# Start-up of a convolution and channel-mix kernel: mu_k loaded earlier, x in four loads, padding zeroed by GpSimd

## The chip, the cores and the metric

The kernel runs on one core of one Trainium2 chip. The metric is device time in microseconds (us) of one execution. "Span" is the time from the first to the last instruction in the profile of one execution, about 1.7 us less than the device time.

Engines: PE is TensorE, PEld its weight loads, DVE is VectorE, ACT is ScalarE, POOL is GpSimd, SP is SyncE; a q behind a name is that engine's queue. "L453" is line 453 of that kernel; the changed kernel's lines are shifted by some five.

## The reference, cut to what matters

```python
# x: (8, 4160, 192); weight: (8 heads, 7 taps)
w = softmax(weight)                                   # per head
y[b, s] = sum over k of w[h, k] * x_padded[b, s + k]  # 6 zero rows in front of every sequence
y_prev = y shifted by one row
xk = mu_k * y + (1 - mu_k) * y_prev
xr = mu_r * y + (1 - mu_r) * y_prev
k = relu(xk @ w_k)                                    # 192 -> 1024
v = (k * k) @ w_v                                     # 1024 -> 192
out = sigmoid(xr @ w_r) * v
```

## The kernel before

The convolution is a matmul with a banded matrix `toe` that is built on the chip from the softmax of the weights. x comes in blocks of 120 rows with 6 rows of overlap, in groups of up to ten blocks. Group 0 is loaded as float32 by the hardware queues and cast by ScalarE, for GpSimd's loads (which cast on their way) start later (the first issue at 2.38 us, against 0.80 us on the hardware queues). The first six groups are the first pair of sequences; group 5 is the first that ends in a partly filled block.

```python
def x_tile(g, eng):                       # eng is always VectorE in this kernel
    p, blk0, nb, _, _ = groups[g]
    xb = three.tile([P, GB, 2, D], BF16, tag="xb", name="xb")     # ring of three buffers
    xbs[g] = xb
    if blk0 == 0:
        eng.memset(xb[0:32, 0, :, :], 0.0)          # zero rows ahead of a sequence
    elif g > 5:
        eng.memset(xb[0:1, 0, 0, 0:2], 0.0)         # one word: VectorE takes the wait for the buffer
    if blk0 + nb == NBLK:
        eng.memset(xb[:, nb - 1, :, :], 0.0)        # the last, partly filled block

def load_x_first(s, eng):                 # three loads for each of two sequences
    nb = groups[0][2]
    for q0, q1, n0, n1 in ((0, P, 1, nb), (16, P, 0, 1), (HALO, 16, 0, 1)):
        eng.dma_start(...)

def softmax():                            # w_raw -> w_max -> w_exp -> ... -> w_nrm
    ...
    for s in range(2):                    # ScalarE casts the first x on the way
        nc.scalar.copy(out=xbs[0][:, : groups[0][2], s, :], in_=x_f32[:, :, s, :])
    ...

def prologue():
    nc.sync.dma_start(out=w_raw, ...)     # the conv weights, to all 128 partitions
    ...
    load_x_first(0, nc.sync)
    load_x_first(1, nc.scalar)
    ...
    load_x(1)
    load_wk()
    warm(..., WARM)                       # 16 matmuls on zeros
    ...
    softmax()
    make_toe()
    load_x(2)
    for i, m in enumerate((moe_mu_k, moe_mu_r)):     # three loads each
        nc.sync.dma_start(out=mu[:, i, 0:1], in_=m[0:P])
        ...
    conv(0, 0)
    tr_first()       # transposes, then d = y - y_prev and xk = mu_k * d + y_prev, c = 0, 1, 2
    conv(1, 0)
    ...
```

After the prologue each bundle of work runs k = wk x xk (PE), relu from PSUM to `k_sb` (ACT, four buffers), square (DVE, frees the buffer), and later v = wv x k (PE).

Of the kernel before, what the change touches and what calls it, by code (L numbers as in the profile page):

```python
# [14 lines left out]
def kernel(  # L15
# [11 lines left out]
    nc = tc.nc  # L27

    B, S, D = x.shape
# [3 lines left out]
    P = 128  # L33
    NF = DF // P
    LO = D - P
    HALO = K - 1
    BLK = 120
# [44 lines left out]
    groups = []  # L82
# [10 lines left out]

    xbs = {}

    def x_tile(g, eng):
        p, blk0, nb, _, _ = groups[g]
        xb = three.tile([P, GB, 2, D], BF16, tag="xb", name="xb")
        xbs[g] = xb
        if blk0 == 0:  # L100
            eng.memset(xb[0:32, 0, :, :], 0.0)
        elif g > 5:

            eng.memset(xb[0:1, 0, 0, 0:2], 0.0)
        if blk0 + nb == NBLK:
            eng.memset(xb[:, nb - 1, :, :], 0.0)

    def load_x(g):
        p, blk0, nb, _, _ = groups[g]
        xb = xbs[g]  # L110
        for s in range(2):
            b = 2 * p + s
            lo, hi = 0, nb
            if blk0 == 0:
                lo = 1
                nc.gpsimd.dma_start(out=xb[HALO:P, 0, s, :], in_=x[b, 0 : P - HALO, :])
            t0 = blk0 * BLK - HALO
            if blk0 + nb == NBLK:
                hi = nb - 1
                r0 = t0 + hi * BLK  # L120
                nc.gpsimd.dma_start(out=xb[0 : S - r0, hi, s, :], in_=x[b, r0:S, :])
            nc.gpsimd.dma_start(  # L122
                out=xb[:, lo:hi, s, :],
                in_=bass.AP(
                    tensor=x.tensor,
                    offset=x.offset + (b * S + t0 + lo * BLK) * D,
                    ap=[[D, P], [BLK * D, hi - lo], [1, D]],
                ),
            )

    def load_x_first(s, eng):

        nb = groups[0][2]
        for q0, q1, n0, n1 in ((0, P, 1, nb), (16, P, 0, 1), (HALO, 16, 0, 1)):
            eng.dma_start(
                out=x_f32[q0:q1, n0:n1, s, :],
                in_=bass.AP(
                    tensor=x.tensor,
                    offset=x.offset + (s * S + n0 * BLK - HALO + q0) * D,
                    ap=[[D, q1 - q0], [BLK * D, n1 - n0], [1, D]],  # L140
                ),
            )



    x_f32 = three.tile([P, NF * STEP], FP32, tag="k2", name="x_f32")[:, 0 : groups[0][2] * 2 * D].rearrange(
        "p (n s d) -> p n s d", s=2, d=D
    )
# [16 lines left out]
    mu = const.tile([P, 2, 2], FP32)  # L165
# [8 lines left out]
    def load_wk():  # L174
        nc.gpsimd.dma_start(out=wk[:, 0, :], in_=moe_w_k[0:P, :])
        nc.gpsimd.dma_start(out=wk[0:LO, 1, :], in_=moe_w_k[P:D, :])
        nc.gpsimd.dma_start(out=wk[LO:P, 1, :], in_=moe_w_k[P:D, :])
# [7 lines left out]
    def load_wv():  # L185
        nc.gpsimd.dma_start(out=wv, in_=moe_w_v.rearrange("(f p) d -> p f d", p=P))

    def softmax():
        nc.vector.tensor_reduce(out=w_max, in_=w_raw, axis=mybir.AxisListType.X, op=ALU.max)
        nc.vector.tensor_tensor(  # L190
            out=w_exp, in0=w_raw, in1=w_max.unsqueeze(2).to_broadcast([P, H, K]), op=ALU.subtract
        )
        nc.scalar.activation(out=w_exp, in_=w_exp, func=AF.Exp)

        nc.scalar.activation(out=w_sig, in_=w_exp[:, 0, 0:1], func=AF.Sigmoid)
        xbs[0] = three.tile([P, GB, 2, D], BF16, tag="xb", name="xb")
        for s in range(2):
            nc.scalar.copy(out=xbs[0][:, : groups[0][2], s, :], in_=x_f32[:, :, s, :])
        nc.vector.tensor_reduce(out=w_sum, in_=w_exp, axis=mybir.AxisListType.X, op=ALU.add)
        nc.vector.reciprocal(out=w_sum, in_=w_sum)  # L200
        nc.vector.tensor_tensor(
            out=w_nrm,
            in0=w_exp,
            in1=w_sum.unsqueeze(2).to_broadcast([P, H, K]),
            op=ALU.mult,
        )

    def masks_mod8():
        for i in range(2):
            nc.vector.tensor_reduce(  # L210
                out=mod8[:, 8 * i : 8 * i + 8],
                in_=ident.rearrange("p (c r) -> p r c", r=8),
                axis=mybir.AxisListType.X,
                op=ALU.add,
            )

    def masks_band():
        nc.gpsimd.affine_select(
            out=band, in_=ones_t, pattern=[[-1, P]], compare_op=ALU.is_ge, fill=0.0, base=0, channel_multiplier=1
        )  # L220
        nc.gpsimd.affine_select(
            out=band, in_=band, pattern=[[1, P]], compare_op=ALU.is_ge, fill=0.0, base=K - 1, channel_multiplier=-1
        )
# [31 lines left out]
    def chunks(g):  # L255
        n = max(1, min(3, BANK // (2 * G * groups[g][2])))
        return [range(h, min(H, h + n)) for h in range(0, H, n)]
# [385 lines left out]
    early, first, xt, mixes, vq, vo, late = ({} for _ in range(7))  # L643

    def at(table, b, fn, *a):
        table.setdefault(b, []).append((fn, a))

    def conv(g, c):
        if g < 3:
            act_, dve_ = nc.scalar.copy, nc.vector.tensor_copy  # L650
            return conv_small(g, (act_, act_, dve_ if g == 0 else act_))
        conv_mm(g, c)
        for k in range(c, min(c + 2, len(chunks(g)))):
            conv_out(g, k, nc.scalar.copy)

    for g, (p, blk0, nb, fb, on_pe) in enumerate(groups):
        nx = 1 if g < 3 else -(-len(chunks(g)) // 2)
        if g == 0:
            continue
        if g == 1:  # L660
            xs = []
        elif p == 0:
            xs = {2: [0], 3: [1, 1], 4: [2, 2, 3, 3], 5: [4, 4, 5, 5]}[g]
        else:
            xs = range(fb - 10, fb - 10 + nx)
        for i, b in enumerate(xs):
            at(xt, b, conv, g, 2 * i)
        if on_pe:
            for j in range((nb + 3) // 4):
                at(first, g - 1, tr, g, j)  # L670
        else:
            at(late, xs[-1], y_write, g)

            at(late, xs[-1] + (1 if g == 4 else 2), y_read, g)
        if g > 3:

            b = {4: 1, 5: 1, 6: 2, 7: 8, 8: 10, 9: 13}.get(g)
            b = first_bundle[first_step[p]] + (-17, -13, -7, -4)[(g - 6) % 4] if b is None else b
            at(early, b, x_tile, g, nc.vector)
            at(early, b, load_x, g)  # L680
    for s, (p, t0, L, n0, ns) in enumerate(steps):
        fb = first_bundle[s]
# [29 lines left out]
    def warm(ps, n):  # L712
        for i in range(n):
            nc.tensor.matmul(out=ps[:, i % 2, :], lhsT=ones_t, rhs=zeros, start=True, stop=True)

    def prologue():
        nc.sync.dma_start(
            out=w_raw,
            in_=bass.AP(tensor=weight.tensor, offset=weight.offset, ap=[[0, P], [K, H], [1, K]]),
        )  # L720
        nc.vector.memset(x_f32[0:32, 0, :, :], 0.0)
        nc.vector.memset(ones_t, 1.0)
        load_x_first(0, nc.sync)
        load_x_first(1, nc.scalar)
        nc.scalar.preload_act_table(AF.Exp)
        nc.vector.memset(zeros, 0.0)
        x_tile(1, nc.vector)
        nc.gpsimd.affine_select(
            out=ident,
            in_=ones_t,  # L730
            pattern=[[1, P]],
            compare_op=ALU.is_equal,
            fill=0.0,
            base=0,
            channel_multiplier=-1,
        )
        masks_band()
        load_x(1)
        load_wk()

        warm(ring.tile([P, 2, BANK], FP32, tag="k", name="warm"), WARM)
        x_tile(2, nc.vector)
        nc.vector.memset(wr[:, 2:4, :], 0.0)
        masks_mod8()
        softmax()
        make_toe()
        load_x(2)
        for i, m in enumerate((moe_mu_k, moe_mu_r)):
            nc.sync.dma_start(out=mu[:, i, 0:1], in_=m[0:P])
            nc.sync.dma_start(out=mu[0:LO, i, 1:2], in_=m[P:D])  # L750
            nc.sync.dma_start(out=mu[LO:P, i, 1:2], in_=m[P:D])
        conv(0, 0)
        tr_first()
        conv(1, 0)
        x_tile(3, nc.vector)
        load_x(3)
        load_wr()
        load_wv()
        for t in tails:
            nc.gpsimd.memset(t, 0.0)  # L760
# [55 lines left out]
```

## Time and profile before

| | before |
|---|---|
| device time, three runs at first | 444.8, 445.12, 445.2 us |
| span of the profiled execution | 443.1 us |
| PE busy | 434.1 us, 98% |
| first relu | 14.07 us |
| first long run of ps_v | 28.40 us |

The page, the chain of waits and the wait for mu_k are shown in the prediction. Columns of the timeline rows: start, length in us, engine, line, operation, output and inputs, shapes, count; in brackets the idle time before the row and what ended it.

```profile
4.46 0.21 DVE L189 TENSOR_REDUCE w_max<-w_raw 128x8 f32<-128x56 f32 x1 [1.94 <-DMA w_raw<-in_weight_dram]
...
14.92 1.90 POOL L122 DMA_DIRECT2D xb<-in_x_dram  x2
15.50 0.63 DVE L431 TENSOR_SCALAR xk<-d,mu 128x1024 bf16<-128x1024 bf16 x1
16.78 0.35 DVE L431 TENSOR_SCALAR xk<-d,mu 128x512 bf16<-128x512 bf16 x1
...
22.27 0.48 DVE L431 TENSOR_SCALAR xr<-d,mu 128x1024 bf16<-128x1024 bf16 x1
22.29 0.94 POOL L122 DMA_DIRECT2D xb<-in_x_dram  x1
23.39 0.35 DVE L431 TENSOR_SCALAR xr<-d,mu 128x512 bf16<-128x512 bf16 x1
24.12 2.49 DVE L536 TENSOR_TENSOR k<-k_sb 128x1024 bf16<-128x1024 bf16 x4
25.30 3.97 ACT L517 ACTIVATE k_sb<-ps_k 128x1024 bf16<-128x1024 f32 x4
28.40 2.80 PE L565 MATMUL ps_v<-wv,k 128*128 128x192 bf16 x32 [0.60 <-ACT k_sb L517]
```

The reader is to see two load issues of GpSimd (a POOL row with DMA_DIRECT2D is GpSimd writing out one load) that begin at 14.92; four tensor_scalar rows of DVE that take 0.63, 0.35, 0.48 and 0.35 us; the fifth square that starts at 24.12 and ends at 24.80; and a relu row at 25.30 that shows no idle time before it.

### The profile page before, as it was taken

The page shows a single profiled execution, that of the slowest core. Times are in us where ns is not written, and L with a number is a line of the kernel's source. Part 1 is how long each engine was busy: PE and PEld are TensorE (multiplying, and loading weights), DVE is VectorE, ACT ScalarE, POOL GpSimd, SP SyncE. Part 2 cuts the span into 40 slices and gives each one's busy share as a digit, 9 for nine tenths or more (in the row PEclk, how much of TensorE's full clock was granted, in tenths as well). Part 3 has the DMA queues.
Part 4 walks back from the last instruction along what each step waited for, and adds up shares of the span by engine and source line. Part 5 has one row for each costly group of instructions (what it writes and reads, how often), then busy time and mean ns, then how long its engine had stood idle before and what let it go on. Part 6 is the DMA issues. An engine that isn't in the chain of part 4 may idle for free.

```text
span 443.1 us, 9799 instructions
## 1 busy us (share of the span) xinstructions
PE 434.1 (98%) x3952; PEld 304.7 (69%) x3952; DVE 388.8 (88%) x704; ACT 354.4 (80%) x462; POOL 44.6 (10%) x64
## 2 busy tenths in 40 slices
PE   8889999999999999999999999999999999999996
PEld 3566776676776776677676677677676677666776
DVE  6899789889988989889978988889988898999973
ACT  5778878889887788888888788888989778877772
POOL 6550001102020100102020000010200000000000
PEclk9999999999999999999999999999999999999999
DMA  7997749969595794295798493476954553422123
GB/s 130 189 165 149 179 135 187 156 170 199 143 219 165 129 195 112 73 207 139 152 210 167 120 219 115 111 113 167 198 155 121 163 131 103 111 73 69 40 72 118
DMA packets 133208, 63.94 MB, mean 144 GB/s; under 512 B 83990, under 2 KB 132906, under 8 KB 133162
## 3 DMA queue, kind: packets, MB, share of 16 engines
q1 hardware_dynamic: 95014, 48.38, 41.2%
q0 software_dynamic: 37360, 14.39, 27.8%
q8 instruction: 31, 0.51, 0.4%
q10 hardware_dynamic: 788, 0.54, 0.4%
q14 instruction: 15, 0.12, 0.1%
HBM read 29.39 MB, written 36.99 MB: 150 GB/s over the span
## 4 chain that ended last, share of the span: by engine, by line
PE 88%; DVE 4%; DMA 3%; ACT 3%; issue 1%; SPq 0%; DVEq 0%; ACTq 0%
PE ps_v L565 38%; PE ps_k L453 37%; PE ps_r L560 4%; PE ps_r L561 4%; PE ps_c L270 4%; DMA mu<-in_moe_mu_k_dram 2%; DVE k L536 2%; ACT y L312 1%; DMA x_f<-in_x_dram 1%; ACT k_sb L517 1%; PE ps_vt L565 1%; DMA xb<-in_x_dram 1%; ACT r_sb L582 0%; DVE d L390 0%; DVE xk L434 0%
## 5 line engine op out<-in xcount | busy, mean ns | idle before, releaser
L517 ACT ACTIVATE k_sb<-ps_k 128x1024 bf16<-128x1024 f32 x260 | 246.1, 1038 | 13.7 <-PE ps_k L453 10.5
L453 PE MATMUL ps_k<-xk,wk 128*128 128x512 bf16 (+3 forms) x1048 | 190.7, 374 | 2.0 <-ACT k_sb L517 0.6
L565 PEld LDWEIGHTS <-k 128*128 128x128 bf16 x2048 | 170.9, 98 | 14.9 <-issue 0.7
L565 PE MATMUL ps_v<-wv,k 128*128 128x192 bf16 x2048 | 179.4, 246 | 0.6 <-ACT k_sb L517 0.6
L536 DVE TENSOR_TENSOR k<-k_sb 128x1024 bf16<-128x1024 bf16 x256 | 168.1, 686 | 10.2 <-ACT k_sb L517 9.1
L453 PEld LDWEIGHTS <-wk 128*128 128x128 bf16 (+1 forms) x1048 | 66.0, 96 | 101.1 <-issue 56.8
L592 DVE TENSOR_TENSOR o_sb<-ps_v,r_sb 128x768 f32<-128x768 f32 x63 | 60.2, 956 | 23.9 <-PE ps_v L565 23.5
L582 ACT ACTIVATE r_sb<-ps_r 128x768 bf16<-128x768 f32 x64 | 53.2, 831 | 24.8 <-PE ps_r L561 24.8
L312 ACT CAST y<-ps_c 120x480 bf16<-120x480 f32 (+4 forms) x78 | 36.2, 523 | 31.3 <-PE ps_c L270 31.3
L122 POOL DMA_DIRECT2D xb<-in_x_dram x34 | 30.8, 910 | 171.6 <-PE ps_k L453 95.0
L560 PE MATMUL ps_r<-wr,xr 128*128 128x192 bf16 x256 | 47.4, 246 | 0.5 <-ACT k_sb L517 0.3
L561 PE MATMUL ps_r<-wr,xr 128*128 128x192 bf16 x256 | 47.4, 246 | 0.0
L434 DVE TENSOR_TENSOR xr<-xr,yT 128x1024 bf16<-128x1024 bf16 (+1 forms) x66 | 36.2, 549 | 2.3
L434 DVE TENSOR_TENSOR xk<-xk,yT 128x1024 bf16<-128x1024 bf16 (+1 forms) x64 | 35.5, 555 | 2.2
L390 DVE TENSOR_TENSOR d<-yT 128x1536 bf16<-128x1536 bf16 (+3 forms) x39 | 31.9, 819 | 0.1
L270 PE MATMUL ps_c<-xb,toe 128*128 128x480 bf16 (+2 forms) x120 | 28.8, 338 | 0.3 <-ACT k_sb L517 0.3
L431 DVE TENSOR_SCALAR xk<-d,mu 128x1024 bf16<-128x1024 bf16 (+1 forms) x64 | 27.1, 424 | 1.1
L561 PEld LDWEIGHTS <-xr 128*128 128x128 bf16 x256 | 25.0, 98 | 4.4 <-DVE xr L431 0.5
L560 PEld LDWEIGHTS <-xr 128*128 128x128 bf16 x256 | 25.0, 98 | 3.5
L431 DVE TENSOR_SCALAR xr<-d,mu 128x1024 bf16<-128x1024 bf16 (+1 forms) x66 | 27.1, 411 | 0.0
L315 ACT CAST y<-ps_c 120x480 bf16<-120x480 f32 (+4 forms) x41 | 19.0, 514 | 8.0 <-PE ps_c L270 8.0
L270 PEld LDWEIGHTS <-toe 128*128 128x128 bf16 x120 | 10.9, 98 | 1.4 <-issue 0.5
(71 smaller groups left out, 90.1 us busy)
## 6 DMA issues: line engine op xcount, KB each, us to landing
out_dram<-o_sb SPq DMA_DIRECT2D x61, 384.0 KB, 2.7
y_dram<-y SPq DMA_DIRECT2D x10, 900.0 KB, 7.0
xb<-in_x_dram POOLq DMA_DIRECT2D x14, 480.0 KB, 8.2
xb<-in_x_dram POOLq DMA_DIRECT2D x6, 432.0 KB, 7.5
xb<-in_x_dram POOLq DMA_DIRECT2D x10, 192.0 KB, 6.8
y_dram<-y SPq DMA_DIRECT2D x3, 450.0 KB, 4.1
y_dram<-y SPq DMA_DIRECT2D x1, 810.0 KB, 5.5
xb<-in_x_dram POOLq DMA_DIRECT2D x2, 384.0 KB, 6.2
```

Of the source, the lines that this page charges most:

```text
L270: nc.tensor.matmul(out=ps[:, :, :, i * G : (i + 1) * G], lhsT=toe[:, h, :], rhs=xbs[g][:, :nb, :, h * G : (h + 1) * G], start=True, stop=True,
L312: copy(out=yh[:, :, :, c0 : c0 + n], in_=ps[:BLK, :, :, 0:n])
L431: nc.vector.tensor_scalar(out=o, in0=d[:, sl, :L], scalar1=mu[:, i, part : part + 1], scalar2=None, op0=ALU.mult)
L434: nc.vector.tensor_tensor(out=o, in0=o, in1=yT[:, sl, c0 : c0 + L], op=ALU.add)
L453: nc.tensor.matmul(out=ps[:, i, f * L : (f + 1) * L], lhsT=wk[r, 0 if hi else 1, fs], rhs=xk[r, i if hi else 2, :L], start=start and f == ...
L517: nc.scalar.activation(out=k_sb, in_=ps.rearrange("p a b -> p (a b)"), func=AF.Relu)
L536: nc.vector.tensor_tensor(out=o, in0=i, in1=i, op=ALU.mult)
L560: nc.tensor.matmul(out=o, lhsT=hi, rhs=wr[:, 0, :], start=True, stop=False)
L561: nc.tensor.matmul(out=o, lhsT=lo, rhs=wlo, start=False, stop=True)
L565: nc.tensor.matmul(out=o, lhsT=k2s[s][:, f, t * P : (t + 1) * P], rhs=wv[:, f, :], start=(f == 0), stop=(f == NF - 1),)
L582: nc.scalar.activation(out=r_sbs[s, j], in_=ps, func=AF.Sigmoid)
L592: nc.vector.tensor_tensor(out=o_sb.rearrange("p (b t) d -> p b (t d)", b=2), in0=v_ps.pop((s, j)), in1=r_sbs.pop((s, j)), op=ALU.mult,)
```

## The change

The intent: mu_k's second and third parts were issued late, so they are put ahead; to make room, the first x comes in four loads; and VectorE is to be spared the zeroing.

```diff
-    def x_tile(g, eng):
+    def x_tile(g):
 ...
+        if g > 4:
+
+            nc.vector.memset(xb[0:1, 0, 0, 0:2], 0.0)
         if blk0 == 0:
-            eng.memset(xb[0:32, 0, :, :], 0.0)
-        elif g > 5:
-
-            eng.memset(xb[0:1, 0, 0, 0:2], 0.0)
+            nc.gpsimd.memset(xb[0:32, 0, :, :], 0.0)
         if blk0 + nb == NBLK:
-            eng.memset(xb[:, nb - 1, :, :], 0.0)
+            nc.gpsimd.memset(xb[:, nb - 1, :, :], 0.0)
 ... (load_x_first takes a queue and one piece; load_mu(i, m) holds the three mu loads)
-        load_x_first(0, nc.sync)
-        load_x_first(1, nc.scalar)
+        for st in range(2):
+            load_x_first(nc.scalar, 0, P, 1, groups[0][2], st, st + 1)
+        load_x_first(nc.sync, 16, P, 0, 1, 0, 2)
+        load_mu(0, moe_mu_k)
+        load_x_first(nc.scalar, HALO, 16, 0, 1, 0, 2)
 ...
-        for i, m in enumerate((moe_mu_k, moe_mu_r)):
-            nc.sync.dma_start(out=mu[:, i, 0:1], in_=m[0:P])
-            nc.sync.dma_start(out=mu[0:LO, i, 1:2], in_=m[P:D])
-            nc.sync.dma_start(out=mu[LO:P, i, 1:2], in_=m[P:D])
+        load_mu(1, moe_mu_r)
```

More of the change, by code (lines that the diff above doesn't have):

```diff
@@ L129, in load_x, with load_x_first, load_mu @@
             )
-    def load_x_first(s, eng):
-        nb = groups[0][2]
-        for q0, q1, n0, n1 in ((0, P, 1, nb), (16, P, 0, 1), (HALO, 16, 0, 1)):
-            eng.dma_start(
-                out=x_f32[q0:q1, n0:n1, s, :],
-                in_=bass.AP(
-                    tensor=x.tensor,
-                    offset=x.offset + (s * S + n0 * BLK - HALO + q0) * D,
-                    ap=[[D, q1 - q0], [BLK * D, n1 - n0], [1, D]],
-                ),
-            )
+    def load_x_first(eng, q0, q1, n0, n1, s0, s1):
+        rows = [[D, q1 - q0]]
+        rest = [[BLK * D, n1 - n0]] if n1 - n0 > 1 else [[S * D, s1 - s0]]
+        eng.dma_start(
+            out=x_f32[q0:q1, n0:n1, s0, :] if n1 - n0 > 1 else x_f32[q0:q1, n0, s0:s1, :],
+            in_=bass.AP(
+                tensor=x.tensor,
+                offset=x.offset + (s0 * S + n0 * BLK - HALO + q0) * D,
+                ap=rows + rest + [[1, D]],
+            ),
+        )
+    def load_mu(i, m):
+        nc.sync.dma_start(out=mu[:, i, 0:1], in_=m[0:P])
+        nc.sync.dma_start(out=mu[0:LO, i, 1:2], in_=m[P:D])
+        nc.sync.dma_start(out=mu[LO:P, i, 1:2], in_=m[P:D])
     x_f32 = three.tile([P, NF * STEP], FP32, tag="k2", name="x_f32")[:, 0 : groups[0][2] * 2 * D].rearrange(
@@ L678 @@
             b = first_bundle[first_step[p]] + (-17, -13, -7, -4)[(g - 6) % 4] if b is None else b
-            at(early, b, x_tile, g, nc.vector)
+            at(early, b, x_tile, g)
             at(early, b, load_x, g)
@@ L722, in prologue @@
         nc.vector.memset(ones_t, 1.0)
-        load_x_first(0, nc.sync)
-        load_x_first(1, nc.scalar)
+        for st in range(2):
[3 more added lines that the diff above has]
+        load_x_first(nc.scalar, HALO, 16, 0, 1, 0, 2)
         nc.scalar.preload_act_table(AF.Exp)
         nc.vector.memset(zeros, 0.0)
-        x_tile(1, nc.vector)
+        x_tile(1)
         nc.gpsimd.affine_select(
@@ L741, in prologue @@
         warm(ring.tile([P, 2, BANK], FP32, tag="k", name="warm"), WARM)
-        x_tile(2, nc.vector)
+        x_tile(2)
         nc.vector.memset(wr[:, 2:4, :], 0.0)
@@ L754, in prologue @@
         conv(1, 0)
-        x_tile(3, nc.vector)
+        x_tile(3)
         load_x(3)
```

## The prediction

> **What bounds the kernel now.** I read the page of the kernel before first: the busy shares, then the 40 slices.
>
> ```profile
> PE 434.1 (98%) x3952; PEld 304.7 (69%) x3952; DVE 388.8 (88%) x704; ACT 354.4 (80%) x462; POOL 44.6 (10%) x64
> ...
> PE   8889999999999999999999999999999999999996
> DVE  6899789889988989889978988889988898999973
> ```
>
> TensorE (PE) is busy for 98% of the span; only the first slices, 33 us, are below nine tenths. A table of stretches puts PE at 40.00 us of 40.00 from 60 to 100 us and at 99.8 to 99.9 of each 100 after that. So the body is a chain of matmuls, and a cheaper instruction on VectorE (DVE) or GpSimd (POOL) buys nothing there. What the change can move is when the chain gets going. So I read the chain that ended last over its first microseconds:
>
> ```profile
> 0.80 4.31 DMA x_f<-in_x_dram
> 5.12 0.02 issue
> 5.13 0.58 SPq L750
> 5.71 0.04 issue
> 5.76 7.22 DMA mu<-in_moe_mu_k_dram
> ```
>
> Columns: start, length, what. The chain goes from a load of the first x to the issue of the second mu_k load (L750, the SyncE queue), then for 7.22 us through the third mu_k load, which lands at 5.76 + 7.22 = 12.98. The wait list of the SyncE queue says why the issue was late, and the timeline of DVE and PE who paid:
>
> ```profile
> SPq L750 <- DMA x_f<-in_x_dram: 2.1, 1, 2.1
> ```
>
> ```profile
> 11.84 0.29 DVE L390 TENSOR_TENSOR d<-yT 128x256 bf16<-128x256 bf16 x1
> 13.10 0.49 DVE L410 SCALAR_TENSOR_TENSOR xk<-d,mu,yT 128x256 bf16<-128x256 bf16 x1 [0.97 <-DMA mu<-in_moe_mu_k_dram]
> 13.50 0.97 DVE L357 COPY yT<-ps_t 128x720 bf16<-128x720 bf16 x2
> ```
>
> ```profile
> 11.33 1.24 PE L478 MATMUL ps_k<-xk,wk 128*128 128x256 bf16 x8
> 12.41 0.80 PE L348 MATMUL ps_t<-ident,y_small 120*128 120x120 bf16 x12
> 13.64 2.13 PE L453 MATMUL ps_k<-xk,wk 64*128 64x256 bf16 x24 [0.43 <-DVE xk L410]
> ```
>
> ```profile
> 14.07 3.77 ACT L517 ACTIVATE k_sb<-ps_k 128x1024 bf16<-128x1024 f32 x4 [2.26 <-PE ps_k L453]
> ```
>
> Square brackets hold the idle time before an instruction and its releaser. DVE idled 0.97 us for mu_k; PE idled only 0.43 us of that, for it had twelve transposes to do meanwhile; ScalarE (ACT) got its first relu at 14.07 and is busy without a gap until 29.
>
> **What the Trainium skill says.** (1) "DMA: Bandwidth & Descriptors", section "Anatomy of one DMA — SWDGE (gpsimd) path", has a fixed cost of about 2.0 us plus bytes at 436 GB/s, so some 2 us for mu_k's 0.2 to 0.5 KB. The trace differs: 5.0 us (first part, issued at 2.68) and 7.1 and 7.2 us (the others). (2) The same page, "Issuing engines are not separate DMA queues": all queues interleave on 16 engines. The trace agrees: between 6 and 8 us GpSimd's queue holds 97.5% of them and SyncE's 0.7%. That is why late tiny loads are slow and why earlier ones should not be. (3) "VectorE: DVE Perf Modes", "Zero memsets can be issued as uint32": one cycle per element. The trace: 218 ns for 192 words, 59 ns for one word, so most of a memset does go with its elements. (4) "SBUF — State Buffer", "Who interferes with whom": a DVE operation in a two-port mode and GpSimd shut each other out. The trace fits: the tensor_scalar at 29.81, beside GpSimd's load issues, took 0.67 us; elsewhere this shape takes 0.48.
>
> **The change part by part.**
>
> *mu_k earlier.* Today the SyncE queue issues the weights, three x loads and the first part of mu_k (2.68); the second part is the ninth such load of the program and is held 2.1 us. With x in four loads instead of six, weights + four x + three mu_k are eight, so I expect no hold. One issue takes about 0.4 us: 0.80 weights, 1.25 x, then mu_k at about 1.7, 2.1, 2.5. With the 5.0 us that today's first part took, the last lands by about 7.5, at worst 9. The first use is at 10.33 and the one that waits today can run at 12.13. So the wait goes: 0.97 us of DVE time.
>
> *What that is worth on PE.* The third xk ends at 12.13 + 0.49 = 12.62. PE's transposes end at 12.41 + 0.80 = 13.21; the last part of wk lands at 5.08 + 7.7 = 12.8. The latest of these is PE itself: L453 starts at 13.2 instead of 13.64, a gain of **0.43 us and no more**. Before that PE has no gap since 1.8 us, so nothing can start sooner.
>
> *Does it carry on?* The first relu moves from 14.07 to about 13.65, and ACT, the busiest engine until 29, moves with it. DVE's copies at 13.50 need ten of the twelve transposes, about 12.41 + 10 x 0.067 + 0.1 = 13.2, so DVE gains 0.3 to 0.4, a little less than ACT. The x of group 2 lands at about 14.8 and its matmuls would run at 15.3 instead of 15.7: still no wait. After 35 us PE is full and carries the shift to the end.
>
> *First x in four loads.* Same bytes. The ACT queue carries 192 + 192 + 15 = 399 KB instead of 284, with the piece every first cast needs behind it. Today the measured loads land at 5.1 to 6.2; I put the last at 6.3 to 6.9. The casts start at 6.63, held by a table load (5.22 + 1.28) and w_sig, not by x. Slack to the conv at 7.96, and 0.5 us more where L478's weight load waits for wk at 11.33, absorb it. Worth 0.
>
> *Zeroing by GpSimd.* Three 32-partition memsets and four 128-partition ones leave DVE (7 x 0.218 = 1.53 us); four one-word ones come (13 instead of 9, 4 x 0.059 = 0.24). Net 1.3 us of DVE, but all but two lie where PE is full. Those at 21.23 and 26.59 become one word each, 0.32 us in the stretch where DVE and ACT set the pace; ACT leads, so I count 0 to 0.1. GpSimd pays some 0.4 us each (its 128x512 memset of tail takes 0.5), before loads needed 15 us or more later. It may hold a two-port DVE operation; I count 0 to 0.1 against.
>
> Sum: 445.12 - 0.43 +/- 0.1 = 444.7 us.
>
> **The rivals.** *A: the wait was hidden anyway, gain 0.* The ring of PSUM tiles is freed by ACT, and PE waits 0.3 us several times for k_sb between 17 and 23. For: PE sat at the ACT pace there. Against: ACT itself idled 2.26 us just for these matmuls, so its row starts sooner. Time 445.1. *B: a transfer takes over.* wk's last part lands 0.4 us before the new start, and the earlier mu_k and mu_r packets share the engines with wk and group 2. 0.4 us later on wk takes the whole gain: 445.1; more, or a late first x, 445.4. Against: some 250 four-byte packets are a small share (276 packets of SyncE's queue took 17% of the engines in 2 us, 5.4 engine-us of 32, 20 ns each). *C: VectorE is the real pace to 28 us.* The chain does run through DVE from 13.10 to 26.02. Then its whole 0.97 + 0.32 might show: 443.9. Against: its copies cannot start before the transposes, so at most 0.4 of the 0.97 counts. *D: GpSimd's zeroing stalls DVE.* 0.2 us lost twice, 445.0; seven zeroings late in the program matter to no matmul.
>
> **Range and chances.** All rivals lie between 443.9 and 445.4. The three runs of before spread over 0.4 us, about the size of the effect. I take 444.7, with 444.2 to 445.2 eight times in ten. Two per cent is 8.9 us, twenty times what is argued, and no wait before the body is a quarter as long: within 2% at 0.98, 0.01 for each side.
>
> **What would show each step right or wrong.** In the changed kernel the SyncE queue's wait for x_f ahead of mu_k is gone, mu_k lands before 9 us, DVE's 0.97 us wait at L410 is gone. L453's 64-row matmuls start at 13.1 to 13.3 and the first relu at 13.6 to 13.7; the long run of ps_v (28.40) starts at 27.9 to 28.1. PE's busy time is unchanged. Wrong if L453 waits for wk or x instead, if the casts start after 7.2 and push the conv, if the first ps_v stays at 28.4, or if GpSimd's later issues make a load late for a group's matmuls.

## The result, and the profile after

| | before | changed |
|---|---|---|
| first measurement, median of 4 | 445.16 us (444.8 to 445.57) | 445.39 us (444.7 to 445.41) |
| ratio, 95% interval | | 1.0001 (0.9984 to 1.0019) |
| second, 5 rounds (9 of before), chip 8 | 444.72 us | 444.82 us |
| third, 5 rounds (9 of before), chip 12 | 444.74 us | 444.90 us |
| span of the profiled execution | 443.1 us | 443.0 us |

A ratio is the mean time of one kernel's fast runs over that of the other's in the same rounds, so it is not quite the ratio of the medians in the table. The time is the same; the argued 0.43 us is not there in any of the three measurements.

The busy line of the changed kernel's page; compare it with the prediction's first fence:

```profile
PE 430.1 (97%) x3889; PEld 304.3 (69%) x3952; DVE 389.4 (88%) x701; ACT 354.5 (80%) x462; POOL 47.8 (11%) x71
```

PE's 4 us less are not work saved: 63 matmul records are missing from this trace, while PEld has all 3952 weight loads in both. DVE did not get lighter either (389.4 against 388.8 us), although three memsets net left it.

The wait list of the SyncE queue, and the rows of the changed kernel's timeline that answer to the mu_k wait:

```profile
SPq L145 <- DMA x_f<-in_x_dram: 2.5, 1, 2.5
```

```profile
12.32 0.48 DVE L415 SCALAR_TENSOR_TENSOR xk<-d,mu,yT 128x256 bf16<-128x256 bf16 x1
13.30 2.29 PE L458 MATMUL ps_k<-xk,wk 64*128 64x256 bf16 x24
13.73 3.77 ACT L522 ACTIVATE k_sb<-ps_k 128x1024 bf16<-128x1024 f32 x4 [1.55 <-PE ps_k L458]
```

mu_k is now issued at 1.74, 2.24 and 2.86 us without a hold and lands at 7.05, 7.23 and 8.79; the hold of 2.5 us has passed to mu_r, whose first part is now the ninth load. VectorE no longer waits for mu_k. The first relu starts 0.34 us earlier. The chain of waits then begins elsewhere, with the conv weights:

```profile
0.80 4.01 DMA w_raw<-in_weight_dram
...
7.50 0.56 DVE toe L249
```

And these rows answer to the ones shown of before:

```profile
15.08 1.93 POOL L122 DMA_DIRECT2D xb<-in_x_dram  x2
15.41 0.90 DVE L436 TENSOR_SCALAR xk<-d,mu 128x1024 bf16<-128x1024 bf16 x1
16.94 0.49 POOL L106 MEMSET xb<- 128x384 bf16 x1
16.96 0.62 DVE L436 TENSOR_SCALAR xk<-d,mu 128x512 bf16<-128x512 bf16 x1
...
22.02 0.90 POOL L122 DMA_DIRECT2D xb<-in_x_dram  x1 [3.74 <-DVE xb L102]
22.51 0.64 DVE L436 TENSOR_SCALAR xr<-d,mu 128x1024 bf16<-128x1024 bf16 x1
23.45 0.90 POOL L122 DMA_DIRECT2D xb<-in_x_dram  x1
23.80 0.66 DVE L436 TENSOR_SCALAR xr<-d,mu 128x512 bf16<-128x512 bf16 x1
24.84 2.49 DVE L541 TENSOR_TENSOR k<-k_sb 128x1024 bf16<-128x1024 bf16 x4
25.62 3.77 ACT L522 ACTIVATE k_sb<-ps_k 128x1024 bf16<-128x1024 f32 x4 [0.36 <-DVE k L541]
28.52 2.80 PE L570 MATMUL ps_v<-wv,k 128*128 128x192 bf16 x32 [0.60 <-ACT k_sb L522]
```

The same four tensor_scalar rows take 0.90, 0.62, 0.64 and 0.66 us, 1.01 us more in all than 0.63, 0.35, 0.48 and 0.35. The fifth square starts at 24.84 instead of 24.12, a relu now waits 0.36 us for a buffer that this square frees, and the first long ps_v starts at 28.52 instead of 28.40. The 0.34 us gained at the relu are gone, and 0.12 more.

### The profile page after: what moved, and what is told of

Its sections match the earlier page's. It is cut to its first block, busy times and chain, and to the rows that moved or that the text cites. A ratio compares the mean times of both kernels' runs of the same rounds, so it can differ in the third digit from the quotient of the medians.

```text
span 443.0 us, 9733 instructions
## 1 busy us (share of the span) xinstructions
PE 430.1 (97%) x3889; PEld 304.3 (69%) x3952; DVE 389.4 (88%) x701; ACT 354.5 (80%) x462; POOL 47.8 (11%) x71
## 4 chain that ended last, share of the span: by engine, by line
PE 88%; DVE 6%; ACT 3%; issue 2%; DMA 1%; DVEq 0%; ACTq 0%
PE ps_v L570 38%; PE ps_k L458 36%; PE ps_r L565 4%; PE ps_r L566 4%; PE ps_c L275 4%; DVE k L541 2%; ACT y L317 2%; DMA w_raw<-in_weight_dram 1%; ACT k_sb L522 1%; PE ps_vt L570 1%; DVE xk L436 1%; DVE xr L436 0%; ACT r_sb L587 0%; ACT y L320 0%; DVE d L395 0%
## 5 line engine op out<-in xcount | busy, mean ns | idle before, releaser
L458 PE MATMUL ps_k<-xk,wk 64*128 64x512 bf16 (+3 forms) x986 | 187.0, 374 | 5.5 <-DVE xk L439 0.7
L436 DVE TENSOR_SCALAR xk<-d,mu 128x1024 bf16<-128x1024 bf16 (+1 forms) x64 | 28.0, 437 | 1.1
L436 DVE TENSOR_SCALAR xr<-d,mu 128x1024 bf16<-128x1024 bf16 (+1 forms) x66 | 28.0, 424 | 0.0
```

Of the source, the lines that this page charges most:

```text
L436: nc.vector.tensor_scalar(out=o, in0=d[:, sl, :L], scalar1=mu[:, i, part : part + 1], scalar2=None, op0=ALU.mult)
L458: nc.tensor.matmul(out=ps[:, i, f * L : (f + 1) * L], lhsT=wk[r, 0 if hi else 1, fs], rhs=xk[r, i if hi else 2, :L], start=start and f == ...
```

## The experiments

The theory after this reading: from 14 to 28 us VectorE and ScalarE run side by side, and the first long ps_v waits for the later of the two. The change moved ScalarE 0.34 us ahead but put VectorE behind, because its tensor_scalar rows are held while GpSimd zeroes a block or writes out a load. The rival: the weights (w_raw), first used at 4.83 instead of 4.46 us, took the gain. Fourteen runs were made, repeats included, with five rounds each (nine of the kernel before beside them); all gave correct results.

The marks of every look, in us. "w" is the start of the first operation on w_raw (w_max), "relu" the first relu, "square" the end of the fifth square, "ps_v" the first long run of it, "end" the span. "Time" is the median of the five rounds, beside that of the kernel before in the same job. The last column is the later of relu + 14.33 and square + 3.00.

| kernel | w | relu | square | ps_v | end | time / before | later of two |
|---|---|---|---|---|---|---|---|
| before | 4.46 | 14.07 | 24.80 | 28.40 | 443.1 | | 28.40 |
| before, again | 4.49 | 13.84 | 24.60 | 28.18 | 442.9 | 444.77 / 444.72 | 28.17 |
| before, third | 4.66 | 13.97 | 24.77 | 28.30 | 443.0 | 444.78 / 444.74 | 28.30 |
| changed | 4.83 | 13.73 | 25.52 | 28.52 | 443.0 | | 28.52 |
| changed, again | 4.83 | 13.73 | 25.54 | 28.54 | 443.0 | 444.82 / 444.72 | 28.54 |
| changed, third | 5.31 | 14.21 | 26.00 | 29.00 | 443.5 | 444.90 / 444.74 | 29.00 |
| 1: changed loads, zeroing on VectorE | 4.77 | 13.67 | 24.85 | 28.01 | 442.5 | 444.29 / 444.72 | 28.00 |
| 1, again | 5.20 | 14.10 | 25.28 | 28.43 | 442.9 | 444.61 / 444.68 | 28.43 |
| 2: loads of before, zeroing on GpSimd | 4.56 | 14.05 | 25.37 | 28.39 | 443.1 | 444.93 / 444.72 | 28.38 |
| 3: changed, group 5 on VectorE | 4.95 | 13.85 | 25.02 | 28.18 | 442.7 | 444.64 / 444.83 | 28.18 |
| 4: changed, no word for group 5 | 5.10 | 13.99 | 25.30 | 28.33 | 442.8 | 444.46 / 444.83 | 28.32 |
| 5: as 1, one x load swapped | 5.58 | 14.47 | 25.65 | 28.80 | 443.3 | 444.59 / 444.83 | 28.80 |
| 6: as 1, group 5 zeroed four times | 5.39 | 14.28 | 26.57 | 29.57 | 444.0 | 445.47 / 444.83 | 29.57 |
| 7: as 1, x behind the weights | 4.92 | 13.82 | 25.00 | 28.16 | 442.5 | 444.19 / 444.68 | 28.15 |
| 7, again | 4.45 | 14.12 | 25.09 | 28.45 | 442.9 | 444.56 / 444.74 | 28.45 |
| 8: as 1, x on the other queue | 4.72 | 13.62 | 24.81 | 27.95 | 442.4 | 444.51 / 444.68 | 27.95 |

The two constants are read off: relu to ps_v is 14.33 to 14.34 wherever ScalarE is the later, square to ps_v 3.00 in the changed kernel. With them the last column meets the measured ps_v in all sixteen rows within 0.01 us; VectorE is the later in four of them (the changed kernel's three looks and experiment 6).

### The kernel before, timed against itself

No edit. Expected:

> The kernel before, unchanged, timed against itself: how far times and the marks of the start-up differ with nothing changed. If the marks are properties of the kernel, the weights (w_raw) land within 0.1 us of 4.4, the first relu starts at 14.0 to 14.1 and the first long ps_v at 28.3 to 28.5; ratio within 0.1% of 1. If the later w_raw of the changed kernel (4.8) is chance, this run can show it too.

The ratio was 1.0000 (0.9988 to 1.0013), w_raw was used at 4.49 as before, but the relu came at 13.84 and ps_v at 28.18, 0.22 us earlier than in the first look: a miss for both marks. The relu stands 0.97 us behind the start of the third xk in all three looks at this kernel (12.87, 13.00 and 13.10 us), and that xk starts when mu_k has landed. So mu_k's landing, and with it the whole body, moves by 0.2 us with nothing changed. What follows: single times decide nothing here.

### The changed kernel again

No edit. Expected:

> The changed kernel, unchanged. Theory (VectorE sets the pace from 14 to 28 us and its two-port tensor_scalar operations are held while GpSimd zeroes or issues loads): first relu near 13.7, the tensor_scalar rows at 15.4 and 17.0 again 0.2 to 0.3 us longer than before, first long ps_v at 28.4 to 28.6; ratio 0.999 to 1.001. Rival (the later w_raw is what cost): if w_raw lands at 4.4 this time, ps_v starts at 28.0 to 28.2.

Every mark came back within 0.02 us, and the long rows with them (0.91, 0.62, 0.64, 0.67 us). Theory and rival were not yet told apart, for w_raw was at 4.83 again.

### 1: the changed loads, zeroing back on VectorE

```diff
-        if g > 4:
+        if blk0 == 0:
+            nc.vector.memset(xb[0:32, 0, :, :], 0.0)
+        elif g > 5:
             nc.vector.memset(xb[0:1, 0, 0, 0:2], 0.0)
-        if blk0 == 0:
-            nc.gpsimd.memset(xb[0:32, 0, :, :], 0.0)
         if blk0 + nb == NBLK:
-            nc.gpsimd.memset(xb[:, nb - 1, :, :], 0.0)
+            nc.vector.memset(xb[:, nb - 1, :, :], 0.0)
```

> The changed loads, but the zeroing back on VectorE as before. Theory: the hold beside the zeroing at 16.9 is gone (0.27 us), the first long ps_v starts 0.2 to 0.4 us earlier than in the changed kernel, 28.1 to 28.3, time 0.05 to 0.1% below. Rival (w_raw): no change against the changed kernel, ps_v at 28.5.

Rows of its timeline:

```profile
15.35 0.91 DVE L436 TENSOR_SCALAR xk<-d,mu 128x1024 bf16<-128x1024 bf16 x1
16.91 0.35 DVE L436 TENSOR_SCALAR xk<-d,mu 128x512 bf16<-128x512 bf16 x1
...
22.32 0.48 DVE L436 TENSOR_SCALAR xr<-d,mu 128x1024 bf16<-128x1024 bf16 x1
22.42 0.90 POOL L122 DMA_DIRECT2D xb<-in_x_dram  x1
23.44 0.35 DVE L436 TENSOR_SCALAR xr<-d,mu 128x512 bf16<-128x512 bf16 x1
...
24.95 3.93 ACT L522 ACTIVATE k_sb<-ps_k 128x1024 bf16<-128x1024 f32 x4
```

Three of the four rows have their old lengths, the relu at 24.95 waits for no square, ps_v starts at 28.01. The ratio to before is 0.9991 (0.9979 to 1.0004), medians 444.29 and 444.72. The interval includes 1, so the time alone is unclear; the profile shows the 0.53 us against the changed kernel (28.54 to 28.01). w_raw was no earlier than in the changed kernel to speak of (4.77 against 4.83). The theory holds (ps_v gained a little more than expected), and the rival that w_raw took the gain does not. Run once more, this kernel gave:

> All zeroing on VectorE, the changed loads, once more: how much w_raw's landing moves with nothing changed (4.77 the first time; 4.83 to 5.39 in others with the same loads). First relu at the first use of w_raw + 8.9, first long ps_v at relu + 14.33; time 0 to 0.1% below before.

It had w_raw at 5.20 and was 0.41 to 0.43 us later at every mark; median 444.61 against 444.68, ratio 0.9997 (0.9984 to 1.0009). Both sums (use + 8.9, relu + 14.33) held to 0.01 us. So against the changed kernel the gain is real in the marks: counted from the use of w_raw, ps_v starts 23.23 and 23.24 us later in the two looks, against 23.69 to 23.71 in the changed kernel's three. Against the kernel before it is not safe: ps_v at 28.43 is later than in all three looks there (28.18 to 28.40).

### 2: the loads of before, only the zeroing on GpSimd

The x_tile of the change in the kernel before.

> The loads of before, only the zeroing moved to GpSimd. Theory: VectorE loses 0.2 to 0.5 us between 15 and 18, the first long ps_v starts at 28.6 to 28.9, time 0.05 to 0.1% above before. Rival (w_raw): w_raw lands at 4.4 as before, ps_v stays at 28.4, ratio 1.000.

```profile
16.80 0.47 POOL L106 MEMSET xb<- 128x384 bf16 x1
16.80 0.62 DVE L431 TENSOR_SCALAR xk<-d,mu 128x512 bf16<-128x512 bf16 x1
```

VectorE lost 0.57 us by its fifth square (25.37 instead of 24.80; 0.2 to 0.5 had been expected by 18 us, and the two later rows were held too, 0.64 and 0.67 us), but ps_v stayed at 28.39: a miss, and by its number the rival's outcome. Experiment 1 speaks against the rival, so the theory was corrected instead. In the kernel before VectorE had about 0.6 us in hand (24.80 + 3.00 = 27.80 against 28.40), and the zeroing used up just that. Alone the zeroing was free; together with an earlier relu it was not. The time, ratio 1.0006 (0.9992 to 1.0019), says the same within its noise.

### 3: only group 5 zeroed on VectorE

```diff
-        if g > 4:
+        if g > 5:
             nc.vector.memset(xb[0:1, 0, 0, 0:2], 0.0)
 ...
-            nc.gpsimd.memset(xb[:, nb - 1, :, :], 0.0)
+            (nc.vector if g == 5 else nc.gpsimd).memset(xb[:, nb - 1, :, :], 0.0)
```

> The changed kernel, but group 5 alone (the first zeroing, in the start-up) zeroed on VectorE without its one-word memset; the other six zeroings stay on GpSimd. Theory (VectorE and ScalarE run side by side from 14 to 28 us and the later sets the first long ps_v; the zeroing of group 5 and the load issues it shifts put VectorE behind): ps_v at 27.95 to 28.1 as with all zeroing on VectorE, time 0.1% below before. Rival (all seven zeroings cost a little each): only a part of the gain, ps_v as above but the end 0.1 to 0.3 us later than with all on VectorE.

w_raw was 0.18 us later than in experiment 1, relu and ps_v by the same 0.17 to 0.18, and the end too (442.66 against 442.49). So the six other zeroings, left on GpSimd, cost nothing; group 5's carried the loss. ps_v at 28.18 missed the expected range by that shift, and the ratio, 0.9997 (0.9983 to 1.001), shows no gain by itself.

### 4: the one-word memset of group 5 left out

Only `if g > 4:` back to `if g > 5:`; GpSimd still zeroes the block.

> The changed kernel without group 5's one-word memset on VectorE; its block is still zeroed by GpSimd. Splits VectorE's loss: the hold beside the zeroing at 17 stays (0.27 us), the holds at 22.5 and 23.8 (0.16 and 0.31) go if they come from where the load issues fall, for these issue at 17.5 to 21 then. Theory: VectorE's fifth square ends near 25.0, ScalarE sets the pace, ps_v at 28.0 to 28.15, time 0.1% below before. Rival (the GpSimd memset itself is what costs): ps_v at 28.3 to 28.5, time as before.

```profile
17.20 0.50 POOL L106 MEMSET xb<- 128x384 bf16 x1
17.22 0.62 DVE L436 TENSOR_SCALAR xk<-d,mu 128x512 bf16<-128x512 bf16 x1
...
22.77 0.48 DVE L436 TENSOR_SCALAR xr<-d,mu 128x1024 bf16<-128x1024 bf16 x1
...
23.89 0.35 DVE L436 TENSOR_SCALAR xr<-d,mu 128x512 bf16<-128x512 bf16 x1
```

The hold beside the zeroing stayed (0.62). The two later ones are gone, because the load issues moved to 18 to 21 us, where no tensor_scalar was held (the nearest, at 20.63, began 0.67 us into an issue of 0.90). From relu to square VectorE took 11.31 us instead of 11.79, and ps_v came 14.34 after the relu: ScalarE and VectorE tie. So one word on VectorE cost 0.46 us at ps_v. It did so by placing GpSimd's large loads at 22.02 and 23.45 us, right ahead of two tensor_scalar rows. ps_v itself, at 28.33, lay where the rival had put it, because w_raw was late again (5.10): from w_raw's use to ps_v it is 23.22 to 23.24 us here and in experiment 1. The ratio was 0.9993 (0.998 to 1.0005).

### 5: one large x load swapped to the SyncE queue

```diff
-        for st in range(2):
-            load_x_first(nc.scalar, 0, P, 1, groups[0][2], st, st + 1)
-        load_x_first(nc.sync, 16, P, 0, 1, 0, 2)
+        load_x_first(nc.scalar, 0, P, 1, groups[0][2], 0, 1)
+        load_x_first(nc.sync, 0, P, 1, groups[0][2], 1, 2)
+        load_x_first(nc.scalar, 16, P, 0, 1, 0, 2)
```

> All zeroing on VectorE, and one large x load moved from the ScalarE queue to the SyncE queue behind the weights, as in the kernel before. Theory: the weights land later in the changed kernel because more x packets of the ScalarE queue run between theirs; here they land at 4.5 to 4.65 instead of 4.77 to 4.83, the conv starts up to 0.2 us earlier, the first relu at 13.55 to 13.67, gain over the other zeroing-on-VectorE kernel 0 to 0.1 us. Rival (the number of loads or mu_k's packets delay the weights): they land at 4.8 again.

w_raw came at 5.58, the latest of all: a miss. The relu stood 8.89 behind it, ps_v 14.33 behind the relu. The median was 444.59 against 444.83 (ratio 0.9994, 0.9981 to 1.0006), while the profiled run took 445.01: that look was a late one.

### 6: group 5 zeroed four times on VectorE

> All zeroing on VectorE, that of group 5 done four times over: 0.66 us more of VectorE at 21.3, nothing for GpSimd. Theory (later of two): VectorE's fifth square ends at 24.85 + 0.66 = 25.5, ps_v 2.95 later at 28.45, the time as before or 0.05% above. Rival (GpSimd, not VectorE's lateness, is what matters): ps_v stays at 28.0 and the time 0.1% below before.

```profile
21.97 1.19 DVE L107 MEMSET xb<- 128x192 uint32 x4
...
26.66 2.86 ACT L523 ACTIVATE k_sb<-ps_k 128x1024 bf16<-128x1024 f32 x3 [0.85 <-DVE k L542]
```

The four took 1.19 us, not 4 x 0.22, so VectorE lost 0.97 us instead of the expected 0.66; with w_raw 0.62 later and 0.13 on a tensor_scalar the square ended at 24.85 + 1.72 = 26.57, and ps_v started 3.00 later at 29.57. The ratio was 1.0016 (1.0003 to 1.0029), the only interval here that leaves 1. Work on VectorE alone, with no zeroing by GpSimd, costs in the same way, once VectorE is the later of the two.

### 7 and 8: where x queues relative to the weights

In 7 all three large x loads stand behind the weights on the SyncE queue and mu_k is on ScalarE's; in 8 the three are on ScalarE's queue. Both have the zeroing on VectorE.

```diff
 7:
-            load_x_first(nc.scalar, 0, P, 1, groups[0][2], st, st + 1)
+            load_x_first(nc.sync, 0, P, 1, groups[0][2], st, st + 1)
         load_x_first(nc.sync, 16, P, 0, 1, 0, 2)
-        load_mu(0, moe_mu_k)
+        load_mu(0, moe_mu_k, nc.scalar)
         load_x_first(nc.scalar, HALO, 16, 0, 1, 0, 2)
 8: the four lines of 7 with nc.sync and nc.scalar exchanged
```

> All zeroing on VectorE; all three large x loads on the SyncE queue behind the weights, mu_k and the smallest x load on the ScalarE queue. Theory (the last packets of w_raw are held by x packets that the other queue brings at the same time): w_raw lands at 4.2 to 4.5, as in the kernel before or earlier; the conv starts at 7.9 to 8.0, first relu at 13.4 to 13.6, first long ps_v 14.33 later, 27.75 to 27.95; time 0.1 to 0.15% below before. Rival (w_raw's landing is chance from run to run, whatever the queues): 4.8 to 5.5 as in the other runs with four loads.

> The opposite: all three large x loads on the ScalarE queue, the SyncE queue has the weights, mu_k and the smallest x load. Theory: w_raw lands latest of all, 5.0 to 5.8, first relu at w_raw's use + 8.9, time as before or above. Rival (chance): same spread as the other runs, and no difference to the kernel with x behind the weights.

The theory that x packets of the other queue hold w_raw back found no support: 4.92 with x behind the weights, 4.72 with x on the other queue, the reverse of what it asked for. Single looks cannot refute it, though, for looks at one kernel lie up to 0.48 us apart (4.83 and 5.31). Version 7 had the lowest median of all, 444.19 against 444.68 (ratio 0.9987, 0.9975 to 1.0), so it was run again, beside another look at both kernels on one chip:

> The kernel before, unchanged. If the early w_raw belongs to the six loads: first use at 4.4 to 4.6 again, first relu 13.8 to 14.1 (set by mu_k's landing, 12.7 to 13.0). If it is the chip and the moment: 4.7 to 5.4 is as likely, and if above 5.1 the relu would be set by w_raw (use + 8.9).

> The changed kernel, unchanged, beside it. Loads: w_raw's first use at 4.75 to 5.4, first relu at that + 8.9, the fifth square of VectorE at the relu + 11.1, first long ps_v 14.8 after the relu (VectorE sets it), time within 0.1% of before. Chance: w_raw as in the kernel before in the same job.

> x behind the weights and all zeroing on VectorE, once more: 444.0 to 444.5 in all five rounds, ratio to before 0.998 to 0.9995, w_raw's first use 4.6 to 5.0, first long ps_v 14.33 after the first relu.

Before had w_raw at 4.66, the changed kernel at 5.31. Version 7 had it at 4.45, but now its casts waited for x, as its timeline shows:

```profile
7.60 1.25 ACT L203 CAST xb<-x_f 128x576 bf16<-128x576 f32 x2 [0.89 <-DMA x_f<-in_x_dram]
```

So its relu came at 14.12, and its five rounds at 444.15 to 444.82 (444.0 to 444.5 expected): a miss. Its median was 444.56 against 444.74, ratio 0.9991 (0.9978 to 1.0005). It leads in both jobs by 0.2 to 0.5 us, but neither interval is clear of 1. No version here is shown to beat the kernel before by its time.

## Why the prediction was right or wrong

**What bounds the kernel, and mu_k.** Right. The eight loads went without a hold and the ninth was held. VectorE's wait of 0.97 us vanished, the third xk started at 12.32 (expected 12.13) and PE's matmuls at 13.30 (expected 13.2); the relu at 13.73 is just outside the 13.6 to 13.7 named. mu_k landed by 8.79 us (predicted 7.5, at worst 9). These early loads were not quick either (5.0 to 5.9 us), so of the 5.0 us by which the second part landed sooner (12.23 to 7.23) 2.9 came from the earlier issue and 2.1 from a shorter time to landing. Two readings were loose: the last of PE's 40 slices (6) is below nine tenths too, and the chain "through DVE from 13.10 to 26.02" spends 2.35 us of it on a load of x.

**The step that failed: "It may hold a two-port DVE operation; I count 0 to 0.1 against."** The mechanism was named, its size was wrong: counted at 0 to 0.1 us, it cost 0.46 us at ps_v and took more than the 0.34 gained. Rival D (the zeroing stalls VectorE, 445.0 us) was the nearest to what came, but it looked at the zeroing alone. The four tensor_scalar rows took 1.01 us more than before; the shorter memset gave 0.16 back (0.22 to 0.06). Of the 1.01, the first row's 0.27 came with the new loads, not with the zeroing: experiment 1, with all zeroing on VectorE, has it too (0.91 us) and still gained; in the looks at the kernel before this row takes 0.63 to 0.78. The zeroing's own share is the other 0.74 us. The hold comes in two forms. The first is beside the zeroing itself: 0.62 instead of 0.35 us, in the changed kernel and in experiments 2 and 4. The second is beside GpSimd's load issues: a row that comes second waits until shortly before the issue ends. The looks give:

| row starts | issue started, length | row's length | alone | would have begun at issue + |
|---|---|---|---|---|
| before, 15.50 | 14.92, 0.95 | 0.63 | 0.48 | 0.73 |
| before again, 15.27 | 14.78, 0.98 | 0.74 | 0.48 | 0.75 |
| changed, 15.41 | 15.08, 0.99 | 0.90 | 0.48 | 0.75 |
| changed, 22.51 | 22.02, 0.90 | 0.64 | 0.48 | 0.65 |
| changed, 23.80 | 23.45, 0.90 | 0.66 | 0.35 | 0.66 |
| before, 22.27 | 22.29, 0.94 | 0.48 | 0.48 | not held: it began first |
| 1, 22.32 | 22.42, 0.90 | 0.48 | 0.48 | not held: it began first |

(Last column: start + length - length alone - issue start.) So each of these rows waits until 0.65 to 0.75 us into the issue, if it comes second, which is 0.22 to 0.25 us before the issue's recorded end. The whole traces say the same: in the sixteen looks 110 tensor_scalar rows are held beside an issue, and all begin 0.22 to 0.26 us before its recorded end, whether it lasts 0.56 or 1.03 us. Which one comes second is not told by the recorded starts alone: the 81 rows that start within 0.18 us after an issue's start are not held. In experiment 1 the row at 29.42 follows an issue of 29.26 and takes 0.49 us, and here it is the issue that is longer, 1.21 us instead of 1.02. This agrees with the Trainium skill, "SBUF — State Buffer", section "Who interferes with whom", where whoever issues first has the shared ports for its whole instruction and the other waits in full; only, by the figures above, the recorded span of a load issue reaches some 0.2 us beyond the hold at both ends (spans on GpSimd are rough). What the page cannot say is how much that is for a given kernel: here it hangs on a few tenths of a microsecond of placement, and the change moved two issues to just ahead of two rows.

**"ACT leads, so I count 0 to 0.1" for VectorE's share.** Half right. ScalarE did lead in the kernel before, by about 0.6 us at the fifth square. The prediction took that lead as given after the change, though the change moved ScalarE ahead 0.34 us and VectorE back 0.72 at the same place. Rival C (VectorE is the pace) was rejected for a gain, and came true as a loss. Experiments 1, 3 and 4 took VectorE's loss away, or enough of it, and ps_v came 14.33 to 14.34 us after the relu again, instead of 14.79; experiment 6 put a loss on VectorE by other means, and it showed. One of the prediction's own signs of being wrong, a first ps_v that stays at 28.4, came true (28.52).

**"First x in four loads ... Worth 0."** Slightly wrong. The slack that was counted was x's; the loads also moved w_raw. In the kernels with six x loads w_raw was used at 4.46 to 4.66 us (four looks), in those with the four loads of the change at 4.77 to 5.39 (eight looks). From there the chain is rigid: the relu comes 8.89 to 8.91 us behind in every look with four loads but version 7's second. In the changed kernel it cost 0.09 us of the predicted 0.43 (13.73 instead of 13.64). In looks with w_raw above 5.1 it costs as much as mu_k did before; in the changed kernel's third look (5.31) the casts start at 7.48, past the 7.2 that the prediction named as a sign of being wrong. That the four loads of the change go with a later w_raw is seen (version 7's second look, with four loads on other queues, has 4.45); why is open. No run has one without the other of the four loads and the early mu_k, whose issues now stand close behind w_raw's on the SyncE queue, so the two are not told apart. Experiments 5, 7 and 8 gave the explanation that was tried no support, and what moves w_raw between looks at one kernel (4.83 to 5.31) was not found either.

**The sum, for the two first looks.** At the relu -0.34 us (predicted -0.43); at ps_v 28.52 - (13.73 + 14.33) = +0.46 lost to VectorE; from ps_v to the end 414.48 instead of 414.70, -0.22. Together -0.10, as the spans 443.1 and 443.0 say. The last term was not predicted at all. It appears in every kernel with four loads (414.3 to 414.5) and in none with six (414.7), and lies behind the start of VectorE's last multiplication (443.1 - 439.53 = 3.57 against 443.0 - 439.65 = 3.35), in the closing part of the program. Its cause was not tested. Version 7, with as many loads as the changed kernel, has 414.33 and 414.40, the others with four loads 414.47 to 414.49, so the number of loads alone does not set it.

**The range.** The first measurement, 445.39, lies above 445.2; later ones of the same kernel (444.82, 444.90) lie inside. That is the width of the range and not the argument: the time is unchanged because the terms above nearly cancel. The range was built around a gain that is not there and took the spread of three runs for the whole noise; the landings of w_raw and mu_k alone move a run by several tenths.

## What to carry to other kernels

When a wait is taken away, ask which engine is second behind the one that profits, and how much it has in hand at the place where the two meet: the gain ends there. An operation moved to an "idle" GpSimd need not be free for VectorE, even if it is long off every chain; look at what VectorE runs at that moment, and also at when the loads behind it are now issued. And where a change is worth less than the spread of the times, follow fixed distances between marks of the trace over several looks instead of the times.

## What the Trainium skill lacked or had wrong

- "SBUF — State Buffer" (who interferes with whom) names the exclusive ports but gives no size for a tensor_scalar held by a load's issue on GpSimd, and does not say when in the issue the ports are taken. Here a tensor_scalar that comes second starts 0.65 to 0.75 us after the start of a large issue in the start-up rows shown (lost: 0.15 to 0.42 us), always 0.22 to 0.26 us before its recorded end, and one that starts within 0.18 us of the issue's start is not held. Beside a 128x384 zeroing of 0.47 to 0.50 us it starts after 0.27 to 0.30 us (lost: 0.27 us).
- "DMA: Bandwidth & Descriptors" gives about 2.0 us of fixed cost in its section on the loads that GpSimd issues; the loads compared with it here and in the prediction are issued by SyncE. At the start of this kernel these took longer: w_raw (28 KB) 3.6 us before and 4.0 after the change, mu_k's second and third part (some 0.2 KB each) 7.1 and 7.2 us before and 5.0 and 5.9 after.
- No page that I read gives the limit behind the hold of the ninth hardware-queue load: 2.1 us on mu_k's second part before, 2.5 us on mu_r's first part after. In both the hold ends as a load of the first x lands (5.12 and 5.91 us). That it is eight is inferred from these two traces; whether the limit is the chip's or the program's is not shown.
